# Sketched attention, a router and eight experts on one core: expert blocks in four waves beside the attention, in place of one pass behind it

## The chip, the core and the metric

One core of a Trainium2 chip runs the whole program. Its engines are TensorE (PE; PEld are its weight loads), VectorE (DVE), ScalarE (ACT), GpSimd (POOL) and SyncE (SP, which here only issues DMAs). The metric is the device time of one execution in microseconds: 638.33 us for the kernel before, the median of 3 runs (637.64 to 638.45). All data is float32.

## What is computed

Four batches of 1088 tokens with four heads of 32. `phi` maps a head's 32 numbers to 64 products of two 8-wide sketches; attention is `phi(q)` times the sum over tokens of `phi(k) v`, divided by `phi(q)` times the sum of `phi(k)`. The result, 4352 tokens of 128, goes to a noisy top-2 router, and each token to two of eight experts with a hidden width of 1024.

```python
q_p, k_p = (phi(q), phi(k))
num = np.einsum('bhsf,bhfd->bhsd', q_p, np.einsum('bhsf,bhsd->bhfd', k_p, v))
den = np.einsum('bhsf,bhf->bhs', q_p, np.sum(k_p, axis=2))[..., None] + 1e-06
x = (num / den).transpose(0, 2, 1, 3).reshape(B * S, H * D)
noisy_logits = x @ w_gate + np.log1p(np.exp(x @ w_noise)) * noise
top2 = np.argpartition(-noisy_logits, 2, axis=1)[:, :2]
...
h = np.maximum(x[mask] @ w1[e], 0.0)
out[mask] += top2_w[mask, k, None] * (h @ w2[e])
```

## The kernel before, in words

A batch is eight tiles of 128 tokens and a rest of 64; two rests make a tile, 34 tiles in all. `attention(b)` (L694) does one batch: `key_values` (L278) transposes the keys, multiplies them with the sketch, forms `phi` on DVE and the batch's `kv` matrix of 64 by 33 per head; `queries` (L324) does the same for four query tiles at a time and divides; `router` (L364) takes these four tiles, transposes them, multiplies with both router weights, picks the top two on DVE, counts the pairs per expert with two products (L435, L436), and POOL scatters each tile's two weighted copies into the DRAM tensor `xs`, at rows sorted by expert (L453). ScalarE needs an Exp and a Ln table in each call (L393, L395, L424). ACT's queue also clears the DRAM tensor `parts` (L236).

Behind the last of nine router calls, `table` (L458) works out on one partition which expert and which rows each block has: 23 blocks of 256 rows, 21 of 128, and four blocks of 256 of the fullest expert. `ends` (L552) writes eight pieces of padding. Then `blocks` (L617): SP fetches each block's rows and its expert's two matrices of 512 KB (`fetch`, L574; five buffers), TensorE transposes the rows (L596), multiplies with w1 into the PSUM bank `hp` (L673), DVE and ACT take turns to evict it with a ReLU, TensorE multiplies with w2 (L632), and POOL scatters the 128-row results into `parts` (L657). Two evicted groups wait in `later` before their second product is issued. When the four last blocks are under way, `combine` (L601) adds the two parts of each token and stores them, and the four blocks' own results are added to the output by accumulating scatters (L648).

Each engine runs its instructions in order. The framework's scheduler chooses that order at build time; each engine then waits on semaphores for what it reads and for buffers to come free.

## Time and profile before

| what | value |
|---|---|
| median of 3 runs | 638.33 us |
| the profiled execution: time, span | 637.79 us, 636.1 us |
| busy PE, PEld | 469.1 us (74%), 408.6 us (64%) |
| busy DVE, ACT, POOL | 198.5, 119.3, 174.7 us |
| DMA | 80.27 MB, mean 126 GB/s |
| mean granted TensorE clock | 0.80 |

The page gives shares over the whole span; since the span has two halves of a different kind, it is read by stretches. A PE matmul of float32 stands in the trace as two records and a transpose as one. The granted clock is a share of 2.4 GHz, so 0.50 is 1.2 GHz.

### The profile page before, as it was taken

What the parts mean: (1) busy time and instruction counts of PE and PEld (TensorE: products, weight loads), DVE (VectorE), ACT (ScalarE), POOL (GpSimd) and SP (SyncE); (2) the same over time, 40 slices, a digit from 0 to 9 for tenths busy, and PEclk for the clock granted to TensorE, in tenths of its full rate; (3) what the DMA queues carried; (4) which work ended last, traced back from release to release, by engine and by line L of the source; (5) the groups of instructions that cost most, each with busy time, mean ns of one, the idle gap of its engine ahead of it and who ended that gap; (6) DMA issues with size and microseconds to landing.
All of it is one profiled execution on the core that took longest, in us unless ns stands there. A gap on an engine that the chain in (4) does not pass through costs nothing.

```text
span 636.1 us, 8071 instructions
## 1 busy us (share of the span) xinstructions
PE 469.1 (74%) x2781; PEld 408.6 (64%) x2781; DVE 198.5 (31%) x687; ACT 119.3 (19%) x232; POOL 174.7 (27%) x236
## 2 busy tenths in 40 slices
PE   0278547847575757854518999999999999999950
PEld 0275337534563456423307999999999999999950
DVE  3112444152513451155371222222232222223430
ACT  0101330121203120132201222222212122221100
POOL 3300155106330524023420313232222313132016
PEclk9999575566557755656557999999999999999995
DMA  8841010001000100000129977868686867750753
GB/s 213 277 164 35 4 63 30 4 1 34 14 19 1 34 4 30 0 14 21 34 57 323 304 235 207 258 197 257 193 255 205 245 222 236 236 150 9 246 189 29
DMA packets 86296, 80.27 MB, mean 126 GB/s; under 512 B 11875, under 2 KB 76004, under 8 KB 85744
## 3 DMA queue, kind: packets, MB, share of 16 engines
q1 hardware_dynamic: 73152, 65.66, 33.5%
q0 software_dynamic: 5472, 8.96, 4.9%
q10 hardware_dynamic: 7632, 5.15, 2.5%
...
q14 instruction: 18, 0.15, 0.1%
HBM read 63.44 MB, written 16.75 MB: 126 GB/s over the span
## 4 chain that ended last, share of the span: by engine, by line
issue 36%; PE 28%; DVE 12%; POOL 9%; DMA 6%; ACT 5%; ACTq 2%; POOLq 1%; SPq 0%; DVEq 0%
POOL parts L657 8%; PE bank L336 5%; PE bank L304 5%; PE bank L255 4%; PE bank L337 4%; DMA two<-parts 3%; PE bank L374 3%; PE bank L350 2%; PE bank L331 2%; ACT L395 2%; DVE phk L249 1%; ACT qT L334 1%; POOL out_dram L648 1%; DVE x L358 1%; DVE phq L341 1%
## 5 line engine op out<-in xcount | busy, mean ns | idle before, releaser
L673 PE MATMUL hp<-bT,w 128*128 128x256 f32 (+1 forms) x768 | 157.9, 338 | 2.4 <-DMA w<-in_moe_w_dram 2.0
L632 PE MATMUL acc<-w,h 128*128 128x128 f32 x1200 | 158.2, 275 | 0.5 <-DVE h L588 0.5
L632 PEld LDWEIGHTS acc<-w,h 128*128 128x128 f32 x1200 | 154.2, 192 | 6.2 <-DVE h L588 0.6
L673 PEld LDWEIGHTS hp<-bT,w 128*128 128x128 f32 x768 | 116.5, 194 | 9.2 <-issue 2.4
L657 POOL DMA_INDIRECT parts<-y,xb x67 | 65.8, 983 | 196.6 <-DVE y L588 147.9
L453 POOL DMA_INDIRECT xs<-xg,to x68 | 69.3, 1019 | 160.5 <-issue 59.5
L588 DVE TENSOR_SCALAR h<-hp 128x512 f32<-128x512 f32 x80 | 55.2, 691 | 120.2 <-PE hp L673 120.2
L590 ACT ACTIVATE h<-hp 128x512 f32<-128x512 f32 x70 | 41.8, 597 | 123.9 <-PE hp L673 123.9
L435 PE MATMUL bank<-masks,earlier 128*128 128x32 f32 (+1 forms) x18 | 5.4, 394 | 62.5 <-DVE g L427 62.5
L435 PEld LDWEIGHTS bank<-masks,earlier 128*128 128x128 f32 x18 | 4.5, 312 | 63.2 <-issue 63.2
L255 PE MATMUL bank<-sk,kT 128*128 128x64 f32 x136 | 29.8, 419 | 11.8 <-ACT kT L290 11.3
L304 PE MATMUL bank<-vaug,phk 128*128 128x66 f32 x128 | 29.4, 424 | 12.3 <-DVE phk L249 12.3
L255 PEld LDWEIGHTS bank<-sk,kT 128*128 128x128 f32 x136 | 29.6, 333 | 12.5 <-ACT kT L290 11.7
L336 PE MATMUL bank<-qT,sq 128*128 128x512 f32 (+1 forms) x36 | 29.9, 928 | 9.8 <-ACT qT L334 9.7
L304 PEld LDWEIGHTS bank<-vaug,phk 128*128 128x128 f32 x128 | 27.9, 330 | 13.4 <-issue 9.8
L341 DVE TENSOR_TENSOR phq<-qa,bank 128x512 f32<-128x512 f32 (+1 forms) x18 | 11.8, 658 | 59.1 <-PE bank L337 58.9
L337 PE MATMUL bank<-qT,sq 128*128 128x512 f32 (+1 forms) x36 | 27.4, 857 | 0.0
L596 PE MATMUL bank<-ident,xb 128*128 128x128 f32 x75 | 16.3, 277 | 14.0 <-DMA xb<-xs 14.0
L350 PEld LDWEIGHTS bank<-kv,phq 128*128 128x128 f32 (+1 forms) x144 | 18.2, 201 | 10.3 <-DVE phq L341 4.7
L334 ACT COPY qT<-bank 128x512 f32<-128x512 f32 (+1 forms) x18 | 10.1, 562 | 76.6 <-PE bank L331 76.6
L588 DVE COPY bT<-bank 128x256 f32<-128x256 f32 x21 | 8.9, 425 | 42.7 <-PE bank L596 42.7
L350 PE MATMUL bank<-kv,phq 128*128 128x66 f32 (+1 forms) x144 | 19.0, 285 | 3.4 <-DVE phq L341 3.4
...
## 6 DMA issues: line engine op xcount, KB each, us to landing
w<-in_moe_w_dram SPq DMA_DIRECT2D x90, 512.0 KB, 4.7
...
kld<-in_k_dram SPq DMA_DIRECT2D x4, 512.0 KB, 4.9
vld<-in_v_dram SPq DMA_DIRECT2D x4, 512.0 KB, 4.0
qld<-in_q_dram SPq DMA_DIRECT2D x4, 512.0 KB, 4.4
...
```

What stands on the lines that cost most here:

```text
L255: nc.tensor.matmul(ps[:, c0:c0 + H * 2 * R], lhsT=kT, rhs=sk[:, i, :], start=(i == 0), stop=(i == 1))
L304: nc.tensor.matmul(o, lhsT=phk[:, t, hs, :].rearrange("p h f -> p (h f)"), rhs=vaug[:, hs, t, :], start=(t == 0), stop=False)
L336: nc.tensor.matmul(pa[:, 0:w], lhsT=sq[:, 0, :], rhs=qT[:, 0:w], start=True, stop=True)
L337: nc.tensor.matmul(pb[:, 0:w], lhsT=sq[:, 1, :], rhs=qT[:, 0:w], start=True, stop=True)
L350: nc.tensor.matmul(ps[rows, c0:c0 + 2 * A1], lhsT=phq[hp][:, P * i + rows.start:P * i + rows.stop], rhs=kv[:, hp, :], start=True, stop=True)
L374: nc.tensor.matmul(ps[:, 2 * E * i:2 * E * (i + 1)], lhsT=xT[:, P * i:P * (i + 1)], rhs=wgn[:], start=True, stop=True)
L453: disjoint("xs", nc.gpsimd.indirect_dma_start(out=xs[:], out_offset=bass.IndirectOffsetOnAxis(ap=to[:, t:t + 1], axis=0), in_=xg[:, t, :], ...
L588: nc.vector.tensor_scalar_max(o, i, 0.0) if relu else nc.vector.tensor_copy(o, i)
L590: nc.scalar.activation(out=o, in_=i, func=AF.Relu) if relu else nc.scalar.copy(o, i)
L632: nc.tensor.matmul(acc[:, D * c:D * (c + 1)], lhsT=h[:, P * (n * i + c):P * (n * i + c + 1)], rhs=w2[:, j, :], start=(j == 0 and c == 0), ...
L657: disjoint("parts", nc.gpsimd.indirect_dma_start(out=parts[:], out_offset=bass.IndirectOffsetOnAxis(ap=to[:, c, :], axis=0), in_=y[:, D * ...
L673: nc.tensor.matmul(hp[:, P * n * i:P * n * (i + 1)], lhsT=w1[:, P * (j0 + i):P * (j0 + i + 1)], rhs=xT[:, 0:P * n], start=True, stop=True)
```

## The change

The blocks are computed in four waves, each from a table of its own. After batch `b` is routed, `table` counts the pairs that came so far; a number of 128-row blocks is then sure to be full whatever the routing (at most 127 rows per expert are left over), and the wave computes that many: 9, 18, 16, and 32 with all the rest behind the last batch. The blocks are all of 128 rows, each with its own fetch of weights (75 instead of 45); there are four weight buffers, two `hp` banks instead of three, and one evicted group waits in `later` instead of two. `wave(0)` is issued behind attention 2, `wave(1)` behind attention 3, so that the scheduler can mix them.

```diff
+    def full_blocks(tiles):
+        return -(-(2 * P * tiles - E * (P - 1)) // P)
+    WAVES, used = [], 0
+    for d in DONE[:-1]:
+        WAVES.append(full_blocks(d) - used)
+        used += WAVES[-1]
+    LAST = (PAIRS + E * (P - 1)) // P - used
+    OLD = (2 * P * DONE[-2] - P * used + E * (P - 1)) // P
...
-    SP = [mybir.EngineType.SP]
-    IN_RANGE = "counts of pairs, clamped in the table"
-    def number(tab, at, most):
-        return nc.values_load(tab[0:1, at:at + 1], engines=SP, min_val=0, max_val=most,
-                              skip_runtime_bounds_check_because=IN_RANGE)
-    def ends(tab):
-        for e in range(E):
-            r = number(tab, 2 * (NB + NS) + 2 + e, E * CAP - P)
-            disjoint("xs", nc.sync.dma_start(xs[bass.ds(r, P), :], pad[:]))
...
-    def fetch(tab, k, n):
-        if k is not None:
-            e = number(tab, 2 * k, E - 1)
-            r = number(tab, 2 * k + 1, E * CAP)
-            return [(rows(r, n), *weights(e), n, False)]
-        e = number(tab, 2 * (NB + NS), E - 1)
-        r = number(tab, 2 * (NB + NS) + 1, E * CAP - 2 * P * NL)
-        w1, w2 = weights(e)
-        return [(rows(r + 2 * P * i, n), w1, w2, n, True) for i in range(NL)]
...
+    def wave(tab, step, K, spread, old=0):
+        fetched, ready, later = [], [], []
+        done = [0]
+        def fetch(i):
+            e = value(tab, 0, i, E - 1)
+            r = value(tab, 1, i, E * CAP)
...
+            w1 = wpool.tile([P, F], F32, name="w1", tag="w1")
+            w2 = wpool.tile([P, FJ, D], F32, name="w2", tag="w2")
+            nc.sync.dma_start(w1[:], moe_w1[bass.ds(e, 1), :, :].rearrange("o p f -> p (o f)"))
+            nc.sync.dma_start(w2[:], moe_w2[bass.ds(e, 1), :, :].rearrange("o (j p) d -> p (o j) d", p=P))
+            fetched.append((xb, w1, w2))
...
+        def second():
+            acc, h, w2, j0, xb = later.pop(0)
+            for i in range(4):
+                nc.tensor.matmul(acc[:, 0:D], lhsT=h[:, P * i:P * (i + 1)], rhs=w2[:, j0 + i, :],
+                                 start=(j0 + i == 0), stop=(j0 + i == FJ - 1))
+            if j0 + 4 < FJ:
+                return
+            y = ypool.tile([P, D], F32, name="y", tag="y")
+            evict(y[:], acc[:, 0:D], spread=spread)
+            disjoint("parts", nc.gpsimd.indirect_dma_start(
+                out=parts[:], out_offset=bass.IndirectOffsetOnAxis(ap=xb[:, D:XW].bitcast(U32), axis=0),
+                in_=y[:], in_offset=None, bounds_check=PAIRS - 1, oob_is_err=False), int(done[0] >= old))
+            done[0] += 1
...
+        fetch(0)
+        turn_input()
+        for b in range(K):
+            if b + 1 < K:
+                fetch(b + 1)
+            xb, w1, w2, xT, acc = ready.pop(0)
+            for j0 in range(0, FJ, 4):
+                hp = ps_h.tile([P, 512], F32, name="hp", tag="hp")
+                for i in range(4):
+                    nc.tensor.matmul(hp[:, P * i:P * (i + 1)], lhsT=w1[:, P * (j0 + i):P * (j0 + i + 1)],
+                                     rhs=xT[:], start=True, stop=True)
+                h = hpool.tile([P, 512], F32, name="h", tag="h")
+                evict(h[:], hp[:], relu=True, spread=spread)
+                later.append((acc, h, w2, j0, xb))
+                if len(later) > 1:
+                    second()
+                if j0 == 0 and fetched:
+                    turn_input()
+        while later:
+            second()
...
-    order = []
-    for i in range(max(NB, NS)):
-        order += [(i, 2)] * (i < NB) + [(NB + i, 1)] * (i < NS)
-    order.append((None, 2))
-    blocks(tab, order)
+    tabs = []
+    for b in range(B):
+        attention(b, b == 0)
+        tabs.append(table(DONE[b], WAVES[b] if b < B - 1 else LAST, b == B - 1))
+        if b >= LEAD:
+            wave(tabs[b - LEAD], b - LEAD, WAVES[b - LEAD], b == B - 1, WAVES[b - LEAD])
+    for b in range(B - LEAD, B - 1):
+        wave(tabs[b], b, WAVES[b], True, WAVES[b])
+    ends(tabs[-1], LAST)
+    wave(tabs[-1], B - 1, LAST, True, OLD)
+    for x in combining["going"]:
+        for _ in x:
+            pass
+    for x in combine(old_tokens, N, 1, 3):
+        for _ in x:
+            pass
```

Combining is done in two parts: the tokens of the first batches while wave 3 runs its newer blocks (`0 < old < K` in `second`), 1152 tokens at the end. The clearing of `parts`, the accumulating scatters and the doubled blocks of the fullest expert are gone.

```diff
+            if 0 < old < K and done[0] > old + 1:
+                todo = combining.setdefault("todo", None)
+                if todo is None:
+                    combining["todo"] = todo = combine(0, old_tokens, 0, G)
+                    combining["going"] = []
+                for x in combining["going"]:
+                    next(x, None)
+                if todo:
+                    combining["going"].append(todo.pop(0))
+                    next(combining["going"][-1])
...
-        for r0 in range(0, per, R_):
-            n = min(R_, per - r0)
-            two = cpool.tile([P, R_, 2, D], F32, name="two", tag="two")
-            behind(nc.sync.dma_start(two[:, 0:n], src[:, r0:r0 + n]), "parts")
-            one = cpool.tile([P, R_, D], F32, name="one", tag="one")
-            nc.vector.tensor_add(out=one[:, 0:n], in0=two[:, 0:n, 0, :], in1=two[:, 0:n, 1, :])
-            disjoint("out", nc.sync.dma_start(dst[:, r0:r0 + n, :], one[:, 0:n]))
...
+        def piece(r0, n):
+            two = work.tile([P, G, 2, D], F32, name="two", tag="phi", bufs=5)
+            behind("parts", nc.sync.dma_start(two[:, 0:n], src[:, r0:r0 + n]), step)
+            yield
+            V.tensor_add(out=two[:, 0:n, 0, :], in0=two[:, 0:n, 0, :], in1=two[:, 0:n, 1, :])
+            yield
+            disjoint("out", nc.sync.dma_start(dst[:, r0:r0 + n, :], two[:, 0:n, 0, :]))
+            yield
+        return [piece(r0, min(C, per - r0)) for r0 in range(0, per, C)]
```

Attention and router are rebuilt. Keys and queries share `features`: a transpose of four tiles of one head, one product with both halves of the sketch, an addition and the products on DVE. The queries' `phi` is transposed afterwards (`attend`), and `kv` is extended by its product with the router's weights, so that the router's logits come out of the same product as the numerators, and the transposes before the router are gone. One ScalarE table that holds Exp and Ln is loaded at the start. The router takes eight or nine tiles in one call (batch 0 in two calls of four): five calls instead of nine. Constants are loaded in two DMAs instead of eight.

```diff
+    def features(tiles, tag, by_head=False):
+        n = len(tiles)
+        ps = bank()
+        for i, x in enumerate(tiles):
+            nc.tensor.transpose(ps[:, P * i:P * (i + 1)], x, ident[:])
+        xT = work.tile([P, 512], F32, name="xT", tag="xT", bufs=3)
+        nc.scalar.copy(xT[:, 0:P * n], ps[:, 0:P * n])
+        ps = bank()
+        for i in range(n):
+            nc.tensor.matmul(ps[:, P * i:P * (i + 1)], lhsT=xT[:, P * i:P * (i + 1)],
+                             rhs=sk[:].rearrange("p i h r -> p (i h r)"), start=True, stop=True)
+        two = ps[:, 0:P * n].rearrange("p (a i b y) -> p a i b y", a=n, i=2, b=H)
+        ab = work.tile([P, G, H, 2, R], F32, name="ab", tag="ab", bufs=3)
+        o = ab[:, 0:n].rearrange("p a b w r -> p b a (w r)" if by_head else "p a b w r -> p a b (w r)")
+        nc.scalar.copy(o, two[:, :, 1])
+        V.tensor_tensor(out=o, in0=two[:, :, 0], in1=o, op=ALU.add)
+        phi = work.tile([P, G, H, RR], F32, name=tag, tag="phi", bufs=5)
+        th = ab[:, 0:n].rearrange("p t h w r -> p (t h) w r")
+        V.tensor_tensor(
+            out=phi[:, 0:n].rearrange("p t h (i j) -> p (t h) i j", i=R),
+            in0=th[:, :, 0, :].unsqueeze(3).to_broadcast([P, H * n, R, R]),
+            in1=th[:, :, 1, :].unsqueeze(2).to_broadcast([P, H * n, R, R]), op=ALU.mult)
...
-            for i in range(n):
-                nc.tensor.transpose(ps[:, P * i:P * (i + 1)],
-                                    qx[:, t0 + i, hp, :, :].rearrange("p c x -> p (c x)"), ident[:])
-            qT = work.tile([P, 512], F32, name="qT", tag="qT")
-            nc.scalar.copy(qT[:, 0:w], ps[:, 0:w])
-            pa, pb = bank(), bank()
-            nc.tensor.matmul(pa[:, 0:w], lhsT=sq[:, 0, :], rhs=qT[:, 0:w], start=True, stop=True)
-            nc.tensor.matmul(pb[:, 0:w], lhsT=sq[:, 1, :], rhs=qT[:, 0:w], start=True, stop=True)
-            qa = work.tile([P, 512], F32, name="qa", tag="qa")
-            nc.scalar.copy(qa[:, 0:w], pa[:, 0:w])
-            ph = work.tile([P, 512], F32, name=f"phq{hp}", tag=f"phq{hp}")
-            nc.vector.tensor_mul(out=ph[:, 0:w], in0=qa[:, 0:w], in1=pb[:, 0:w])
-            phq.append(ph)
...
+        ps = bank()
+        for hp in range(2):
+            nc.tensor.transpose(ps[0:KC, P * hp:P * (hp + 1)], kv[:, hp, 0:KC], ident[:])
+        kvT = work.tile([KC, 2 * P], F32, name="kvT", tag="kvT")
+        nc.scalar.copy(kvT[:], ps[0:KC, 0:2 * P])
+        ps = bank()
+        for hp in range(2):
+            nc.tensor.matmul(ps[:, 2 * E * hp:2 * E * (hp + 1)], lhsT=kvT[:, P * hp:P * (hp + 1)], rhs=wgn[:, hp, :],
+                             start=(hp == 0), stop=True, skip_group_check=True)
+        both = ps[:, 0:4 * E].rearrange("p (a x) -> p a x", a=2)
+        V.tensor_copy(kv[upper, :, KC:KC + 2 * E], both[upper, :, :])
+        nc.scalar.copy(kv[lower, :, KC + 2 * E:YC], both[lower, :, :])
...
+        for hp in range(2):
+            ps = bank()
+            for i in range(n):
+                nc.tensor.transpose(ps[:, P * i:P * (i + 1)], two_heads(phi, i, hp), ident[:])
+            t = work.tile([P, 512], F32, name="phT", tag="phT", bufs=4)
+            nc.scalar.copy(t[:, 0:P * n], ps[:, 0:P * n])
+            phT.append(t)
+        for i0 in range(0, n, 2):
+            m = min(2, n - i0)
+            ps = bank()
+            for i in range(i0, i0 + m):
+                for rows, kv in kvs_of[i]:
+                    for hp in range(2):
+                        c0 = 2 * YC * (i - i0) + YC * hp
+                        nc.tensor.matmul(
+                            ps[rows, c0:c0 + YC], lhsT=phT[hp][:, P * i + rows.start:P * i + rows.stop],
+                            rhs=kv[:, hp, :], start=True, stop=True)
+            nc.scalar.copy(nd[:, at + i0:at + i0 + m].rearrange("p t a y -> p (t a y)"), ps[:, 0:2 * YC * m])
...
+        V.tensor_scalar_add(den, nd[:, 0:n, :, DH:DH + 2], 1e-6)
+        V.reciprocal(den, den)
+        sc = small.tile([P, MOST, H, 2 * E], F32, name="sc", tag="sc")[:, 0:n]
+        V.tensor_tensor(
+            out=sc.rearrange("p t h y -> p (t h) y"),
+            in0=nd[:, 0:n, :, KC:YC].rearrange("p t a (h y) -> p (t a) h y", h=2),
+            in1=den.rearrange("p t a h -> p (t a) h").unsqueeze(3).to_broadcast([P, 2 * n, 2, 2 * E]),
+            op=ALU.mult)
+        V.tensor_add(out=sc[:, :, 0:2, :], in0=sc[:, :, 0:2, :], in1=sc[:, :, 2:4, :])
+        lz = t3("lz", 2 * E)
+        V.tensor_add(out=lz, in0=sc[:, :, 0, :], in1=sc[:, :, 1, :])
+        logits, z = lz[:, :, 0:E], lz[:, :, E:2 * E]
...
-        ps = bank()
-        for i in range(n):
-            nc.tensor.transpose(ps[:, P * i:P * (i + 1)], x[:, i, :, :].rearrange("p h d -> p (h d)"), ident[:])
-        xT = work.tile([P, 512], F32, name="xT", tag="xT")
-        nc.scalar.copy(xT[:, 0:w], ps[:, 0:w])
-        ps = bank()
-        for i in range(n):
-            nc.tensor.matmul(ps[:, 2 * E * i:2 * E * (i + 1)], lhsT=xT[:, P * i:P * (i + 1)],
-                             rhs=wgn[:], start=True, stop=True)
```

Three places of the new order, beside the old one. TensorE, in the middle of the program: before, the tail of the first batch's router and the start of the second batch (`kx` keys, `qx` queries).

```order
L374 MATMUL bank<-wgn,xT 128x16 x4
L435 MATMUL bank<-masks,earlier 128x32
L288 MATMUL bank<-ident,kx 128x128 x7
L436 MATMUL bank<-before,ones 128x32
L288 MATMUL bank<-ident,kx 128x128
L255 MATMUL bank<-sk,kT 128x64 x16
L304 MATMUL bank<-vaug,phk 128x66 x8
L306 MATMUL bank<-vaug_rest,phk_rest 128x66
```

Now, in attention 2 (`vld_106` its values, `kv_172` its matrix, `w_1265`, `w_1266` and `w_1281` weights of wave 0's first two blocks):

```order
L670 MATMUL hp<-bT,w_1265 128x128
L352 MATMUL bank<-vld_106,phk 128x96 x8
L352 MATMUL bank<-v_rest,rest_phi_995 128x96 x2
L640 MATMUL acc<-w_1266,h 128x128 x3
L362 MATMUL bank<-ident,kv_172 66x128 x2
L640 MATMUL acc<-w_1266,h 128x128
L670 MATMUL hp<-bT,w_1281 128x128 x2
L367 MATMUL bank<-wgn,kvT 128x16 x2
L304 MATMUL bank<-ident,qld 128x128 x4
L670 MATMUL hp<-bT,w_1281 128x128 x2
L640 MATMUL acc<-w_1266,h 128x128
L465 MATMUL side<-masks,earlier 128x72
```

Between the products of one batch's attention stand first-layer (L670) and second-layer (L640) groups of wave 0, and a counting product of the router before (L465).

TensorE, late in the blocks (numbers are weight buffers). Before, first-layer (L673) and second-layer (L632) groups alternate, each second-layer group of four behind another first-layer group:

```order
L673 MATMUL hp<-bT,w_3077 128x128 x4
L632 MATMUL acc<-w_3030,h 128x128 x4
L596 MATMUL bank<-ident,xb 128x128 x2
L673 MATMUL hp<-bT,w_3077 128x128 x4
L632 MATMUL acc<-w_3030,h 128x128 x4
L673 MATMUL hp<-bT,w_3135 128x256 x2
L632 MATMUL acc<-w_3078,h 128x128 x4
```

Now, in the last wave, a block's eight first-layer products stand together, and its eight second-layer ones right behind them:

```order
L632 MATMUL acc<-ident,xb 128x128
L670 MATMUL hp<-bT,w_4439 128x128 x8
L640 MATMUL acc<-w_4440,h 128x128 x8
L632 MATMUL acc<-ident,xb 128x128
L670 MATMUL hp<-bT,w_4486 128x128 x8
L640 MATMUL acc<-w_4487,h 128x128 x8
```

POOL: before, all scatters of routed rows (L453) stand ahead of all scatters of block results (L657):

```order
L453 DMA xs<-xg_1625,to_1623 36096x129 x4
L453 DMA xs<-xg_1637,to_1635 36096x129 x4
L453 DMA xs<-xg_1753,to_1751 36096x129 x2
L453 DMA xs<-xg_1763,to_1761 36096x129 x2
L657 DMA parts<-y,xb 8704x128 x67
L648 DMA out_dram<-y,tok 4352x128 x8
```

Now the results of wave 0's second and third block (L646) stand behind the last of the 18 scatters of batch 1 (`xg_898`, `xg_904`), and batch 2's follow behind the next two:

```order
L501 DMA xs<-xg_898,to 35968x129
L501 DMA xs<-xg_904,to 35968x129
L646 DMA parts<-y,xb 8704x128 x2
L491 COPY xg_1892<-pair 128x9
L491 COPY xg_1898<-pair 128x9
L646 DMA parts<-y,xb 8704x128 x2
L501 DMA xs<-xg_1196,to 35968x129
L501 DMA xs<-xg_1202,to 35968x129
```

A block's input buffer, which its result's scatter reads for the row numbers, is free only when that scatter is done.

## Rows read from the trace of the kernel before

**Rows 1.** The page, part 2: the span in 40 slices of 15.9 us.
```profile
PE   0278547847575757854518999999999999999950
...
PEclk9999575566557755656557999999999999999995
DMA  8841010001000100000129977868686867750753
```

**Rows 2.** Windows: stretch, length, busy per engine (instructions), granted clock, DMA share, GB/s.
```profile
104.00:128.00 24.00, 18.99 (x72) 14.28 (x72) 4.12 (x6) 2.93 (x5) 7.77 (x10) 0.58 0.05 17
312.00:332.00 20.00, 2.04 (x9) 1.80 (x8) 15.25 (x106) 3.37 (x6) 6.15 (x7) 0.50 0.17 50
344.28:360.00 15.72, 15.72 (x127) 15.28 (x126) 4.04 (x7) 3.52 (x7) 2.97 (x3) 1.00 1.11 342
360.00:370.93 10.93, 10.93 (x85) 10.52 (x84) 2.92 (x5) 2.32 (x5) 2.95 (x3) 1.00 0.77 239
```

**Rows 3.** Timeline of PE, small block of the steady stretch: start us, us, instructions.
```profile
388.99 1.06 PE L673 MATMUL hp<-bT,w 128*128 128x128 f32 x8
389.89 1.06 PE L632 MATMUL acc<-w,h 128*128 128x128 f32 x8
390.78 0.38 PE L596 MATMUL bank<-ident,xb 128*128 128x128 f32 x2
```

**Rows 4.** Timeline of all engines, first 40 us, idle before in brackets.
```profile
9.29 0.18 DVE L103 TENSOR_SCALAR expo<-words 128x16 uint32<-128x16 uint32 x1 [8.26 <-DMA words<-in_S_dram]
...
18.84 1.97 PE L288 MATMUL bank<-ident,kx 128*128 128x128 f32 x8 [0.74 <-POOL kx L282]
...
32.08 7.09 PE L255 MATMUL bank<-sk,kT 128*128 128x64 f32 x32 [11.27 <-ACT kT L290]
```

**Rows 5.** Timeline, the first router call (four tiles).
```profile
66.23 0.19 DVE L392 SCALAR_TENSOR_TENSOR u<-zs 128x32 f32<-128x32 f32 x1 [3.56 <-ACT zs L391]
...
66.70 1.28 ACT L395 ACT_TABLE_LOAD   x1
...
76.35 0.17 DVE L446 CAST to<-at 128x4 uint32<-128x4 f32 x1
```

**Rows 6.** Timeline of POOL, scatters of the routed rows.
```profile
78.43 0.97 POOL L453 DMA_INDIRECT xs<-xg,to  x1 [0.30 <-issue]
79.70 0.96 POOL L453 DMA_INDIRECT xs<-xg,to  x1 [0.30 <-issue]
```

**Rows 7.** DMA issues: line, count, KB each, median us to landing.
```profile
w<-in_moe_w_dram SPq DMA_DIRECT2D x90, 512.0 KB, 4.7
...
xb<-xs SPq DMA_DIRECT2D x21, 64.5 KB, 4.7
xs<-xg,to POOLq DMA_INDIRECT x68, 2.3
```

**Rows 8.** Timeline of SP's queue behind the table.
```profile
321.79 6.41 SPq L555 DMA_DIRECT2D xs<-pad  x8
332.26 0.42 SPq L568 DMA_DIRECT2D xb<-xs  x1
...
334.66 0.34 SPq L568 DMA_DIRECT2D xb<-xs  x1
```

**Rows 9.** Timeline, eviction of the group that starts at 388.99.
```profile
390.15 0.60 ACT L590 ACTIVATE h<-hp 128x512 f32<-128x512 f32 x1 [2.44 <-PE hp L673]
```

**Rows 10.** The chain that ended last, its end: start us, us, releaser.
```profile
588.39 2.25 DMA parts<-y,xb
590.78 3.88 DMA two<-parts
...
614.48 2.00 DMA out_dram<-one
```

**Rows 11.** Source line 392, one instruction per router call.
```profile
L392 DVE SCALAR_TENSOR_TENSOR u<-zs x9: 191/192/240, 66.2 to 312.7; 128x32 f32<-128x32 f32 x8, 128x16 f32<-128x16 f32 x1
```

766 lines of the change are left out of this document (347 added, 419 removed).

## The prediction

> **What bounds the kernel now.** I read the slices of the span first, then the stretches, then the order of time inside three of them. The slices fall in two halves [rows 1]: up to about 330 us TensorE is busy half to three quarters of the time at a granted clock around 0.6 and the DMA engines are nearly idle; behind it TensorE is full at 1.0 and the DMA engines work. The stretches say the same with numbers [rows 2]: 0.58 while attention runs, 0.50 while the one table is made and TensorE has 2 us of work in 20, 1.00 in the expert blocks. The first half is thus a chain of short steps, the second is TensorE's own pace. The change can gain by putting blocks under the chain, and by a shorter chain; it can't gain in the blocks' own pace.
>
> The pace of a block: groups of four matmuls of 128 columns follow each other at 0.90 and 0.89 us [rows 3]; a 128-row block is four such groups and a transpose of 0.11, so 4 x 0.89 + 0.11 = 3.67 us. Three units (a 256-row and a 128-row block) take 10.93 us [rows 2], 3.64 each: cutting 256 into 128 costs TensorE next to nothing. That is at 2.4 GHz. In the first 40 us the same instructions take twice that: eight transposes 1.97, 16 matmuls (32 records) 7.09 us, so 0.246 and 0.443 each [rows 4]; that is 1.2 GHz, though the slices print 1.0 there, so I go by the durations.
>
> **The change part by part.** Both kernels compute 75 units of 128 rows (before 27 x 2 + 21; after 9 + 18 + 16 + 32). Before, all of them stand behind the table. After, TensorE's order has attention 0 and 1 alone, then wave 0 mixed into attention 2, wave 1 into attention 3, then waves 2 and 3.
>
> (a) Until the first block. The DVE starts its sketch constants at 9.29 us, when eight small loads on ACT have landed [rows 4]; two loads are left, I take 5.5, and first transposes at 10.5. Attention 0 and 1 are 74 transposes and 115 matmuls in the new order: 74 x 0.246 + 115 x 0.443 = 69 us at 1.2 GHz, 35 at 2.4. With some 8 us for the hops of two key chains (copy, transpose, copy, product, copy) that is 10.5 + 69 + 8 = 88. The other condition gives the same: the first four tiles' numerators are there at about 45; a router call takes 10.3 us from its first step to its row numbers for four tiles [rows 5], 2 x 1.28 of it table loads that the one preloaded table removes, but two calls now share DVE with attention 1's features, so the second ends near 70. Then eight scatters at 1.27 [rows 6] behind the first eight, 2.3 to land [rows 7], an input block of 4.7: 70 + 10.2 + 2.3 + 4.7 = 87. I take **88**; ends 68 (2.4 GHz throughout, only the chain) and 105 (1.2 GHz, and TensorE waits at each of the five router products that the order puts between attention 1's). All else that attention loses (the expanded query copies on POOL, the clearing of the parts by 4.4 MB from ACT's queue, the transposes before the router) is inside this count, not beside it.
>
> (b) TensorE's work from there on: 75 x 3.67 = **275**, and attention 2 and 3, 72 transposes and 115 matmuls at 2.4 GHz (half of 0.246 and 0.443), **34**.
>
> (c) Waits inside that, which are mine to choose. In attention 2 TensorE's order holds 17 us of attention and 10 us of blocks, but DVE has router 1, table 1 and ten feature products: a router call of nine tiles between 10.3 and 20.6 us, I take 16, some 5 for a table (DVE's whole load in the 20 us around the old, wider one was 15.25 [rows 2]), 8 for features, and the chain's ends: 40 us in all, so 13 wait. Attention 3 starts behind wave 0 with router 2 done: 6 wait. POOL has block 1's output behind router 1's 18 scatters (18 x 1.27 = 23 us), and wave 1's first input needs a buffer which that output frees: 4. A new wave starts with an empty pipeline, 1.5 each, and the last one behind eight padding writes which take 6.41 us on SP [rows 8] and are only just covered by the four weight buffers: 4 + 3. From the middle of wave 2 the order puts the two first-layer groups ahead of the two second-layer groups; an eviction on ACT starts 0.26 behind the group's end and takes 0.60 [rows 9], on DVE 0.09 more, against 0.89 of cover: about 0.15 in some 40 blocks, 6. Combining the older tokens inside wave 3 moves 4.9 MB, 14 us at 342 GB/s [rows 2], over seven blocks that leave 0.2 us each: 8 after the prefetch lead. Sum **44**, ends 25 and 75.
>
> Feeding the blocks: 75 loads of weights instead of 45, each block 1.05 MB of weights, 0.066 in and 0.066 out: 1.18 MB. Before's own burst moves 342 GB/s for 16 us with TensorE full [rows 2], so 3.45 us per block against 3.67: it hides, by little. SP issues a fetch every 2.4 us [rows 8], which hides too. With 3.67 at 2.4 GHz, the price is nothing as long as the DMA engines give over 321 GB/s. Here a rule of the Trainium skill speaks against the change: "DMA: Bandwidth & Descriptors", section Bandwidth, asks for transfers of 1 MiB and more, and its section on the anatomy of a DMA puts 2.0 us of fixed cost on each. As an estimate from that page, two loads of 512 KB one behind the other would be 6.4 us per block, and the sum some 200 us more. The row says otherwise, since it shows the same 512 KB loads overlapping; I follow the row.
>
> (d) The end. Before, 614 to 636 are eight accumulating scatters; after, the last block's output goes to the parts (0.5 for the copy), from scatter to load 2.25, loads of three pieces 3.9, a store 2.0 [rows 10], an add and issues between: **12** instead of some 22.
>
> Sum: 88 + 275 + 34 + 44 + 12 = 453 us of span. The profiled execution of before had 636.1 of span in 637.79, so 1.7 around it; its time is 0.5 below the median of 638.33, which I leave aside: **455 us**.
>
> **The rivals.**
> 1. The front is quicker: TensorE reaches 2.4 GHz in attention 0 and 1, or half my waits aren't there. For it: no clearing on ACT's queue; against it: 0.58 all through the attention of before [rows 2]. 455 - 20 - 10 = 425.
> 2. The blocks are bound by DMA. Before's steady stretch ran 239 GB/s at 0.77 busy [rows 2], 310 at full; midway between 239 and 342 is 290, 4.07 us per block, 0.4 more in the 64 blocks with no attention beside them: 455 + 25 = 480. Against it: the burst; for it: the burst was short.
> 3. The overlap doesn't come: the in-order engines make the mixed waves wait for attention and the reverse. A batch takes 61.6 us now (eight router calls in 246.5 us [rows 11], two per batch); both mixed stretches at that, with 10 us of blocks each, instead of 40 and 33: 455 + 70 = 525. For it: one TensorE queue, router products in the middle of blocks; against it: nothing in a block depends on the attention beside it.
> 4. Slower: TensorE stays at 1.2 GHz. If every wave has short gaps (late weights, router products), the blocks run at the pace that attention has now. Then (b) doubles, 309 more, and takes up most of (c): about 730. It decides from a mean granted clock of 0.63: 88 + 309 / 0.63 + 44 + 12 + 2 = 637. For it: attention with TensorE 0.79 busy was granted 0.58 [rows 2]; against it: blocks back to back were granted 1.00 without a break. "TensorE: Matmul & The Clock Gate" of the Trainium skill, section on HAM oscillation, describes this case, bursts of matmuls between waits for weights that each run cold; the blocks of before, fed by the same loads, don't show it.
>
> **How the numbers follow.** The forecast 0.64 (its own range 435 to 475), rival 1 0.11, rival 2 0.15, rival 3 0.07, rival 4 0.02, and 0.01 for what lies between 3 and 4, near no change. The range 424 to 500 takes in the first three and leaves rivals 3 and 4 out. A measurement of this kernel tells changes of about 0.2% from none. Faster: 0.64 + 0.11 + 0.15 + 0.07 = 0.97; the same 0.01; slower 0.02.
>
> **What would show it.** Right: the first expert transpose near 88 us; a granted clock at 1.0 from some 130 us to the end; PE full in 40-us stretches with DMA at 300 GB/s or more; blocks 3.7 to 3.9 us apart; wave 3 starting near 305. Wrong: block starts over 4 us apart with TensorE waiting for weights (rival 2); TensorE idle on features or on router products for over 30 us between 88 and 190 (rival 3); a clock near 0.6 in waves (rival 4); or POOL's outputs behind the scatters holding input buffers for more than the 4 us that I gave them.

## The result, and the profile after

The changed kernel takes **434.41 us** (median of 4 runs, 433.68 to 435.31) where the kernel before took 637.99 beside it (636.92 to 638.45): ratio 0.681, 95% interval 0.679 to 0.683. 455 was forecast, with 424 to 500. The same kernel took 494.8 us (ratio 0.771, 0.766 to 0.776) when it ran again among the experiments, with the kernel before unchanged at 639.7; that gap of 60 us is the subject of half the experiments. Times are medians of all executions of a run, one of 1317 us in e7 among them whose cause isn't known; ratios leave out the slow executions, those over 1.5% above the fastest.

The page of the run at 434, span and slices of 10.8 us, for [rows 1]:

```profile
span 433.5 us, 9044 instructions
...
PE   1878782999998999998999999999999999889980
...
PEclk9999796899999999999699999999999999999995
DMA  6193012974959289893999999699999979999915
```

From the eighth slice to the last but one TensorE is 0.8 busy or more, at a granted clock of 0.8 or more but for the twentieth. Stretches of it (columns as in [rows 2]):

```profile
60.00:80.00 20.00, 11.09 (x77) 10.00 (x77) 6.52 (x28) 5.83 (x15) 9.76 (x13) 0.74 0.37 111
100.00:140.00 40.00, 37.64 (x324) 36.29 (x323) 20.24 (x87) 16.22 (x40) 30.99 (x33) 1.00 0.78 244
140.00:180.00 40.00, 39.36 (x338) 37.60 (x337) 24.64 (x88) 13.92 (x36) 19.39 (x19) 1.00 0.71 215
200.00:220.00 20.00, 17.27 (x128) 16.84 (x127) 3.63 (x8) 3.19 (x7) 9.47 (x10) 0.83 0.85 267
220.00:260.00 40.00, 39.67 (x353) 39.27 (x352) 10.52 (x21) 8.90 (x21) 10.81 (x11) 1.00 1.07 339
360.00:380.00 20.00, 17.81 (x144) 16.73 (x145) 6.35 (x13) 3.69 (x10) 5.50 (x5) 1.00 1.05 347
```

From 100 us on TensorE works 37 to 40 us of each 40; only 200 to 220 and the combining from 360 to 400 fall below 18 of 20. At 220 to 260 the DMA engines move 339 GB/s beside a full TensorE, and no block waits for a load.

TensorE's way to the first block (timeline: start, us, idle before in brackets), for [rows 4]:

```profile
10.41 2.08 PE L309 MATMUL bank<-sk,xT 128*128 128x128 f32 x8 [0.68 <-ACT xT L306]
...
26.80 1.16 PE L309 MATMUL bank<-sk,xT 128*128 128x128 f32 x8 [0.73 <-ACT xT L306]
...
36.61 0.60 PE L304 MATMUL bank<-ident,kld 128*128 128x128 f32 x4
...
66.17 0.66 PE L304 MATMUL bank<-ident,kld 128*128 128x128 f32 x4
74.99 0.47 PE L632 MATMUL acc<-ident,xb 128*128 128x128 f32 x1 [8.16 <-DMA xb<-xs]
```

Eight records of a feature product take 2.08 us at 10 and 1.16 at 27: TensorE was at half speed first and at full speed from some 25 us on, in attention 0, though the page prints 1.00 for both. It fell back to half speed twice before the blocks ran: from 48 to 56 (granted 0.57, four transposes 1.09 in place of 0.60 or 0.66) and from 75, behind the 8.2 us wait, to 80. Attention 0 ends at 36.6, attention 1 at 66.2, and then TensorE waits 8.2 us for the first block's rows. POOL says why, for [rows 6]:

```profile
49.47 1.16 POOL L501 DMA_INDIRECT xs<-xg,to  x1 [30.20 <-DVE noisy L455]
...
61.67 0.96 POOL L501 DMA_INDIRECT xs<-xg,to  x1 [0.30 <-issue]
...
70.58 0.97 POOL L501 DMA_INDIRECT xs<-xg,to  x1 [0.30 <-issue]
```

Sixteen scatters follow each other, most of them every 1.27 us, from 49.5 to 71.6. The ninth, the first of the router's second call, starts at 61.67 without a wait: its row numbers had been there since 56.5 (DVE, L484). The last lands at 72.9, the rows are in at 74.9.

Blocks, for [rows 3]. Middle of wave 2, then wave 3, then wave 3 beside the combining:

```profile
242.18 0.83 PE L670 MATMUL hp<-bT,w 128*128 128x128 f32 x6
242.85 0.27 PE L632 MATMUL acc<-ident,xb 128*128 128x128 f32 x1
242.96 0.39 PE L670 MATMUL hp<-bT,w 128*128 128x128 f32 x2
...
307.28 2.05 PE L670 MATMUL hp<-bT,w 128*128 128x128 f32 x16
309.19 1.64 PE L640 MATMUL acc<-w,h 128*128 128x128 f32 x12
310.67 0.27 PE L632 MATMUL acc<-ident,xb 128*128 128x128 f32 x1
...
359.48 0.27 PE L632 MATMUL acc<-ident,xb 128*128 128x128 f32 x1
360.11 2.05 PE L670 MATMUL hp<-bT,w 128*128 128x128 f32 x16 [0.35 <-ACT bT L608]
...
363.94 0.27 PE L632 MATMUL acc<-ident,xb 128*128 128x128 f32 x1
```

From transpose to transpose it is 3.68 (to 246.54), then 4.01 (from 306.66), then 4.46. In the last, the transpose stands behind all of the second layer and the next first layer waits 0.35 for its eviction.

### The profile page after: what moved, and what is told of

Read it like the earlier page. It is cut to its first block, busy times and chain, and to the rows that moved or that the text cites. A ratio compares the mean times of both kernels' runs of the same rounds, so it can differ in the third digit from the quotient of the medians.

```text
span 433.5 us, 9044 instructions
## 1 busy us (share of the span) xinstructions
PE 382.2 (88%) x3089; PEld 363.8 (84%) x3089; DVE 165.4 (38%) x564; ACT 113.3 (26%) x274; POOL 153.5 (35%) x208
## 4 chain that ended last, share of the span: by engine, by line
PE 55%; issue 16%; POOL 9%; DMA 9%; DVE 7%; ACT 2%; SPq 1%; POOLq 0%; ACTq 0%; DVEq 0%
PE hp L670 19%; PE acc L640 18%; POOL xs L501 5%; PE bank L309 5%; POOL parts L646 4%; PE bank L352 4%; PE bank L392 3%; DMA xs<-xg,to 3%; DMA w<-in_moe_w_dram 2%; PE bank L304 2%; DMA xb<-xs 2%; PE acc L632 1%; DMA two<-parts 1%; DMA parts<-y,xb 1%; PE bank L381 1%
## 5 line engine op out<-in xcount | busy, mean ns | idle before, releaser
L670 PE MATMUL hp<-bT,w 128*128 128x128 f32 x1200 | 163.6, 281 | 6.3 <-ACT bT L608 3.6
L640 PE MATMUL acc<-w,h 128*128 128x128 f32 x1200 | 164.3, 282 | 0.1
L670 PEld LDWEIGHTS hp<-bT,w 128*128 128x128 f32 x1200 | 148.3, 194 | 12.0 <-ACT bT L608 8.5
L640 PEld LDWEIGHTS acc<-w,h 128*128 128x128 f32 x1200 | 148.6, 193 | 2.4 <-ACT h L608 0.3
L646 POOL DMA_INDIRECT parts<-y,xb x75 | 75.1, 1002 | 189.7 <-DVE y L606 124.7
L606 DVE COPY y<-acc 128x128 f32<-128x128 f32 x66 | 19.1, 290 | 103.8 <-PE acc L640 96.1
L608 ACT COPY bT<-acc 128x128 f32<-128x128 f32 x75 | 20.0, 266 | 117.3 <-PE acc L632 114.2
L632 PE MATMUL acc<-ident,xb 128*128 128x128 f32 x75 | 21.3, 284 | 12.5 <-DMA xb<-xs 12.0
L309 PE MATMUL bank<-sk,xT 128*128 128x128 f32 x136 | 24.3, 326 | 6.5 <-ACT xT L306 6.5
L309 PEld LDWEIGHTS bank<-sk,xT 128*128 128x128 f32 x136 | 20.4, 226 | 9.7 <-ACT xT L306 9.6
L632 PEld LDWEIGHTS acc<-ident,xb 128*128 128x128 f32 x75 | 10.7, 142 | 14.3 <-DMA xb<-xs 8.4
L315 DVE TENSOR_TENSOR ab<-bank,ab 128x256 f32<-128x256 f32 (+1 forms) x20 | 7.6, 380 | 36.7 <-ACT ab L314 36.6
L392 PE MATMUL bank<-kv,phT 128*128 128x98 f32 (+1 forms) x144 | 18.4, 279 | 1.5 <-ACT phT L383 1.5
L352 PE MATMUL bank<-vld,phk 128*128 128x96 f32 x128 | 17.6, 297 | 0.3 <-DVE phk L318 0.3
L352 PEld LDWEIGHTS bank<-vld,phk 128*128 128x128 f32 x128 | 16.9, 213 | 0.8 <-DVE phk L318 0.5
L306 ACT COPY xT<-bank 128x512 f32<-128x512 f32 (+1 forms) x20 | 10.5, 523 | 10.3 <-PE bank L304 9.6
```

The lines of the kernel that those rows point to most:

```text
L306: nc.scalar.copy(xT[:, 0:P * n], ps[:, 0:P * n])
L309: nc.tensor.matmul(ps[:, P * i:P * (i + 1)], lhsT=xT[:, P * i:P * (i + 1)], rhs=sk[:].rearrange("p i h r -> p (i h r)"), start=True, stop= ...
L352: nc.tensor.matmul(ps[:, W * hp:W * (hp + 1)], lhsT=lhsT, rhs=rhs, start=(t == 0 and hp == 0), stop=(t == NT), skip_group_check=True)
L392: nc.tensor.matmul(ps[rows, c0:c0 + YC], lhsT=phT[hp][:, P * i + rows.start:P * i + rows.stop], rhs=kv[:, hp, :], start=True, stop=True)
L606: V.tensor_scalar_max(o, i, 0.0) if relu else V.tensor_copy(o, i)
L608: nc.scalar.activation(out=o, in_=i, func=AF.Relu) if relu else nc.scalar.copy(o, i)
```

## The experiments

They ran on the chips with the numbers 2 (e1 to e6), 7 (e7 to e9), 10 (e10, e11) and 9 (e12); on which chip the run above ran isn't known. They also ran later, so what is said below of a chip could be the time's doing as well. Ratios are to the kernel before, timed on the same chip in the same rounds.

**e1, the order of waves 2 and 3 pinned as the code has it** (waves 2 and 3; the products of L640 and L670 are pinned in the same way).

```diff
+        keep = tc.keep_in_program_order if pin else (lambda i: i)
...
-            nc.tensor.transpose(acc[:, P:2 * P], xb[:, 0:D], ident[:])
+            keep(nc.tensor.transpose(acc[:, P:2 * P], xb[:, 0:D], ident[:]))
...
```

> Edit: in waves 2 and 3 TensorE's instructions keep the order of the code, in which first-layer and second-layer groups of four alternate and the next block's transpose stands between them; nothing else changes. Theory (the order costs): in the changed kernel a block takes 3.68 us where groups alternate and 4.01 where eight first-layer products stand together, since the eviction is then uncovered; 27 blocks of 4.01 give back 9 us, and the ten blocks beside the combining (45.6 us from 355.0 to 400.6) go to some 39 in place of 45.6. 434.4 becomes 417 to 421. Rival (DMA binds in the last wave): 32 blocks at 1.18 MB, 0.5 MB of padding and 5 MB of combining are 43 MB, 125 us at the 347 GB/s of that stretch, as long as the wave takes now; then the same time goes to waits for weights, and the total stays above 429.

505.6 us, ratio 0.790 (0.786 to 0.795): 11 more than the unedited kernel there (e5); theory and rival were both reckoned from the run at 434. In the code's order the transpose follows the group that ends a bank's use, and waits for its eviction, 4.34 us per block:

```profile
301.80 0.33 PE L634 MATMUL acc<-ident,xb 128*128 128x128 f32 x1 [0.44 <-DVE y L606]
...
306.14 0.33 PE L634 MATMUL acc<-ident,xb 128*128 128x128 f32 x1 [0.44 <-DVE y L606]
```

So a block's pace does follow the order, but this was the wrong order; e6 mends it.

**e2, no overlap** (all four waves behind the loop over attention, pinned; padding behind wave 2's loads).

```diff
-        if b >= LEAD:
-            wave(tabs[b - LEAD], b - LEAD, WAVES[b - LEAD], b == B - 1, WAVES[b - LEAD])
-    for b in range(B - LEAD, B - 1):
-        wave(tabs[b], b, WAVES[b], True, WAVES[b])
...
+    for b in range(B - 1):
+        wave(tabs[b], b, WAVES[b], b > 0, WAVES[b], pin=True)
```

> Edit: all four waves stand behind all four attentions on TensorE, with groups alternating in all of them (so it is compared with e1_alternate, not with the changed kernel). Theory (the gain comes from the shorter attention, and the overlap hides little): attention 1 takes 30 us alone in the changed kernel (36.6 to 66.2), attention 2 and 3 will take 30 to 35 each, so the first block starts at 127 to 137, 75 blocks at 3.68 are 276, and with some 6 of wave starts and 13 of tail the total is 422 to 434: 5 to 15 more than e1_alternate. Rival (the overlap is the bulk of the gain): a batch alone takes the 61.6 us that it took before the change, the first block starts near 190, the total is 480 or more, over 60 above e1_alternate.

531.2 us, 0.832 (0.827 to 0.836), some 25 more than e1. The first block starts at 166.0, where before it started at 334.6. Attention 2 takes 38 us alone and attention 3 42, both with TensorE near half speed for most of the time (windows, granted clock 0.60 and 0.67) and attention 3 with two late completions (8 us), and TensorE then waits 17 us for router 3:

```profile
69.08 1.12 PE L304 MATMUL bank<-ident,kld 128*128 128x128 f32 x4
...
107.05 0.60 PE L304 MATMUL bank<-ident,kld 128*128 128x128 f32 x4
...
148.49 0.73 PE L392 MATMUL bank<-kv,phT 128*64 128x98 f32 x8 [0.92 <-issue]
...
166.00 0.47 PE L635 MATMUL acc<-ident,xb 128*128 128x128 f32 x1
```

```profile
69.00:107.00 38.00, 29.38 (x148) 25.90 (x148) 21.64 (x86) 9.41 (x24) 6.68 (x11) 0.60 0.43 129
107.00:149.00 42.00, 29.96 (x159) 25.91 (x158) 20.97 (x88) 10.43 (x28) 18.82 (x21) 0.67 0.09 29
```

So the first block moves up by 169 us without any overlap: attention and router take about 40 per batch and not 61.6 [rows 11], and the last table isn't waited for by all blocks. The 25 lie between the theory's 5 to 15 and the rival's 60, but they aren't the overlap's worth. The late completions told of under e5 weigh on this pair unequally: ACT waits 66 us for them in e1 (sum of the table of waits) and 26 in e2. And e2 pins the slow order in waves 0 and 1 too, which e1 doesn't: their 27 blocks come 4.25 to 4.41 us apart in e2, so some 16 of the 25 can be the order's (27 times 0.6, the step from 3.68). The first makes the overlap look smaller than it is, the second larger; what it is worth wasn't measured. The two traces show the size of it: in the run at 434, the 101 us from 75 to 176 hold all of attention 2 and 3 and the products of some 15 blocks; in e2, attention 2 and 3 and the last router take 97 us without a block.

**e3, more buffers.**

```diff
-    xpool = ctx.enter_context(tc.tile_pool(name="xpool", bufs=8))
-    ypool = ctx.enter_context(tc.tile_pool(name="ypool", bufs=6))
+    xpool = ctx.enter_context(tc.tile_pool(name="xpool", bufs=16))
+    ypool = ctx.enter_context(tc.tile_pool(name="ypool", bufs=14))
```

> Edit: 16 input buffers for blocks in place of 8, and 14 output buffers in place of 6; nothing else. Theory (input buffers are held by outputs queued on POOL behind the 18 scatters of batch 3, so SP's fetch comes late at 203 us): the two blocks at 199 to 212.6 us, which take 13.4 us in place of 7.4, are back at 3.68 each, without the half-speed clock behind the wait: 6 us, and up to 2 more at other fetches that waited; 434.4 becomes 426 to 429. Rival (the fetch waits for something else, the weight buffers or the scattered rows): no change, 433 to 436.

496.0, 0.771 (0.764 to 0.778): as e5. But the wait that it was to remove isn't in e5's profile either (in the run at 434, SP waits 30.8 us for results to leave input buffers; here that row is missing, and TensorE is late itself). It stays open what the buffers are worth.

**e4, the first block later on TensorE.**

```diff
+            if step == 0:
+                tc.add_manual_dep(t_.ins, last_of[LEAD].ins.name, ORDER, reason="behind the key chain")
```

> Edit: on TensorE the first block's transpose stands behind the key-value product of attention 2, in place of ahead of most of it; nothing else. Theory (the 8.2 us in which TensorE waits for the first block's rows, 66.8 to 75.0, are filled with attention 2's key features and products): 5 to 8 us less, 426 to 430, and the clock doesn't fall in that stretch. Rival (attention 2's own chain on DVE, with the router of batch 1, sets the end of the mixed stretch, so the wait moves there): under 2 us less, 432 to 435.

494.8 (485.3 to 497.7; no ratio), as e5 (490.0 to 495.6): no gain shown. Again the wait isn't there to be filled: in e5 attention 1 itself ends at 78.3, and the first block's transpose follows at 79.2 without a wait for its rows. Open for the same reason.

**e5, no edit.**

> The changed kernel without an edit, to be compared with e1 to e4, which all came out between 494 and 531 us, and in which TensorE's completions reach ACT and SP up to 15 us late while POOL issues the 18 scatters of a batch (e3_pools has the very same order of instructions on every engine as the changed kernel). Theory (a property of the chip or the time that those four ran at, not of their edits): this kernel too takes 485 to 510 here, with TensorE idle for 10 us and more at a time in the bursts of 18 scatters. Rival (the edits did it, through other buffer addresses): 432 to 437 as in the profile after the change.

494.8, 0.771 (0.766 to 0.776). Theory held: the time comes with this chip, or the time at which it ran, and not with an edit. Wave 2's first transpose is at 287.0 in place of 225.7, and from there to the last transpose both runs take the same 190 us (287.0 to 477.2, 225.7 to 416.7): the 61 us lie ahead of wave 2. Four of them are there before the first scatter, which starts at 53.5 in place of 49.5: the feature products at 28 and 32 still take 2.08 us, where the run at 434 had 1.16. The other 57 lie in the stretch with the 68 scatters of routed rows. TensorE, ACT and SP in the first burst beside blocks, and POOL's part:

```profile
106.49 1.08 PE L640 MATMUL acc<-w,h 128*128 128x128 f32 x8
...
113.67 1.58 PE L670 MATMUL hp<-bT,w 128*128 128x128 f32 x8
...
131.18 0.48 PE L632 MATMUL acc<-ident,xb 128*128 128x128 f32 x1 [12.67 <-ACT y L608]
...
110.47 0.27 ACT L608 COPY y<-acc 128x128 f32<-128x128 f32 x1 [2.40 <-remote]
...
130.37 0.60 ACT L608 ACTIVATE h<-hp 128x512 f32<-128x512 f32 x1 [12.86 <-remote]
...
110.46 0.38 SPq L626 DMA_DIRECT2D w<-in_moe_w_dram  x1
...
130.40 0.38 SPq L626 DMA_DIRECT2D w<-in_moe_w_dram  x1
...
109.73 0.97 POOL L501 DMA_INDIRECT xs<-xg,to  x1 [0.30 <-issue]
...
126.27 1.00 POOL L646 DMA_INDIRECT parts<-y,xb  x1 [0.30 <-issue]
```

Second-layer products that the trace puts at 106.5 to 107.6 release ACT's copy and SP's next load together at 110.46, 2.9 us late, and the first-layer group of 113.67, recorded as done by 115.3, releases ACT's next eviction at 130.37, with SP's load again at the same moment. The trace has no event that released them ("remote"). The ends of matmuls are modelled, so it can't be told whether the products or their signals were late. All waits without a releaser are for results or buffers of TensorE; between DVE, ACT and POOL there is none.

**e6, the transpose inside the first-layer group.**

```diff
+                    if pin and j0 == 4 and i == 3 and fetched:
+                        turn_input()
...
-                if j0 == 0 and fetched:
+                if j0 == 0 and fetched and not pin:
```

> Edit: as e1_alternate, but the next block's transpose stands between the third and the fourth product of the second first-layer group, where it stands in the blocks that took 3.68 us; in e1_alternate it stood behind the second-layer group that frees its PSUM bank, and waited 0.44 for that bank's eviction, 4.34 per block. Theory (the order alone sets a block's pace): blocks of waves 2 and 3 at 3.68 to 3.75, where the changed kernel has 4.01, and at most 4.0 beside the combining where it has 4.46; 15 to 20 us less than the changed kernel in the same session. Rival (DMA binds in the last wave): blocks wait for weights, less than 5 us gained.

487.4, 0.764 (0.759 to 0.770), 7 less than e5; the intervals overlap a little, so the gain rests on the traces: from wave 2's first transpose to the last it takes 183.8 in place of 190.3. In waves 2 and 3, 33 of the 47 steps from block to block take 3.68 or 3.69, at 310 to 350 GB/s, so DMA feeds that pace. Less than expected, because eight blocks beside the combining take 38.6 us, 9.1 more than at 3.68; TensorE waits there for rows, 5.1 us in all, and for weights, 1.3:

```profile
414.18 0.30 PE L634 MATMUL acc<-ident,xb 128*128 128x128 f32 x1 [0.51 <-DMA xb<-xs]
...
425.38 0.30 PE L634 MATMUL acc<-ident,xb 128*128 128x128 f32 x1 [1.24 <-DMA xb<-xs]
```

In 420 to 440 the DMA engines moved 371 GB/s at a share of 1.09. Theory for the blocks alone, rival for the combining's stretch.

**e7, plain writes on ACT's queue in place of scatters.** The rows go to fixed places and aren't sorted by expert, so e7 and e11 don't compute the result; they price the scatters and aren't kernels to use.

```diff
-                disjoint("xs", nc.gpsimd.indirect_dma_start(
-                    out=xs[:], out_offset=bass.IndirectOffsetOnAxis(ap=to[:, i, t:t + 1], axis=0),
...
+                m = 2 * (t0 + t) + i
+                r0 = m % E * CAP + m // E * P
+                disjoint("xs", nc.scalar.dma_start(xs[r0:r0 + P, :], xgs[i][:, t, :]), step)
```

> Edit: the routed rows go to DRAM by plain writes of whole tiles from ACT's queue, at fixed rows, in place of the 68 scatters on POOL; blocks read fixed tiles and the padding is at fixed rows (so a block's rows are not those of its expert; the same number of rows, bytes and blocks). Compared with e5_same_again, 494.8, where TensorE's completions reach ACT and SP 2.5 to 15 us late in the bursts of scatters. Theory (POOL's scatters themselves delay the completions): without them no idle TensorE of 10 us beside the attention, 410 to 440 in all. Rival (the writes of 516-byte rows do it, or the chip alone whatever the kernel does): the same stretches stay idle, over 470.

460.6, 0.720 (0.717 to 0.723), and no late completion at all, on the chip on which e9, with its scatters, has them. The time misses the theory's 410 to 440 and rules out the rival's 470; the idle time that is left is the edit's own: ACT stands in front of its writes, and TensorE waits for it (table of waits: total, times, longest):

```profile
ACT bT L608 <- DMA xs<-xg: 29.2, 2, 17.6
```

**e8, the kernel before.**

> The kernel before, without an edit, for its profile on this chip, since its time here (639) is that of the first session while the changed kernel's is 60 us longer. Theory (the late completions come with scatters issued while TensorE works without a break): before's scatters, eight at a time and beside DVE's router, delay completions too, but TensorE waits there for DVE anyway, so the span is within 2 us of 636 and TensorE's busy time in 60 to 330 us is unchanged. Rival (its shorter bursts cause no late completion at all): no wait of ACT or SP for a completion that is over 1 us late.

639.6, span 637.9 (one profile). Its waits show no completion without a releaser. The rival: in this profile bursts of eight, beside a TensorE that is 0.6 busy, delay nothing.

**e9, all combining at the end** (the edit is to e6).

```diff
-    wave(tabs[-1], B - 1, LAST, True, OLD, pin=True)
+    wave(tabs[-1], B - 1, LAST, True, 0, pin=True)
...
-    for x in combine(old_tokens, N, 1, 3):
+    for x in combine(0, N, 1, G):
```

> Edit: as e6_alternate_inside, but all combining stands behind the last block. Compared with e6, 487.4. Theory (beside the blocks the combining costs what DMA can't move: 9 us, eight blocks of 38.6 in place of 29.4 in e6): the wave gets 9 us shorter, and the 2944 older tokens at the end cost 4.5 MB at some 340 GB/s, 13 us, so 2 to 6 us slower than e6. Rival (combining beside blocks is free in e6, the waits come from the weights alone): 11 us or more slower than e6.

494.5, 0.774 (0.770 to 0.779), 7 more than e6 but on another chip, so the traces decide. Wave 3 takes 113.8 from first to last transpose in place of 124.1, what follows the last transpose 34.0 in place of 18.0. So combining costs 10.3 us beside the blocks and 16.0 behind them, 5.7 more there: the theory's 2 to 6, and not the rival's 11. (The tokens that moved are 3200, 4.9 MB, and not the expectation's 2944.)

**e10, gaps on POOL behind the scatters of batches 2 and 3.**

```diff
+                if step >= 2:
...
+                    for g_ in range(3):
+                        gap = nc.gpsimd.memset(fill[:], 0.0)
+                        tc.add_manual_dep(gap.ins, s_.ins.name, ORDER, reason="behind the scatter")
```

> Edit: behind each of the 36 scatters of batches 2 and 3 POOL clears a scratch tile three times (some 1.4 us), and results of blocks may go between them; batches 0 and 1 keep their bursts, as a control in the same run; 16 input and 11 output buffers for blocks, so that the longer queue holds none. Compared with e5_same_again (494.8), where the bursts of batch 2 (140 to 170 us) and batch 3 (225 to 255) cost TensorE some 20 us each in late completions. Theory (it takes scatters back to back to delay completions): no completion over 1 us late beside batches 2 and 3, those of batch 1 as in e5; 450 to 465. Rival (each scatter delays by itself, or as long as scatters are under way): the same waits or longer ones beside batches 2 and 3, 490 or more.

461.7, 0.725 (0.721 to 0.729): 33 less than e5, across two chips. The surer comparison is inside the run, batch 1 against batches 2 and 3. Windows, e5 above and e10 below:

```profile
100.00:140.00 40.00, 22.73 (x161) 21.23 (x160) 15.57 (x75) 9.91 (x24) 20.74 (x23) 0.79 0.40 117
140.00:180.00 40.00, 23.85 (x158) 22.43 (x158) 4.71 (x32) 8.38 (x21) 20.47 (x21) 0.74 0.57 165
```

```profile
100.00:140.00 40.00, 24.47 (x164) 23.33 (x162) 15.79 (x77) 8.72 (x22) 22.44 (x26) 0.70 0.44 130
140.00:180.00 40.00, 39.46 (x338) 37.73 (x337) 12.49 (x24) 16.13 (x42) 36.17 (x51) 1.00 0.61 188
```

The burst of batch 1, left as it was, costs as much as in e5; that of batch 2, with three clearings (1.7 us) between its scatters, nothing any more. The larger buffers aren't the cause: e3 had 16 and 14 and took 496. Two late pairs are left, at 199 (4.6 and 4.0 us) and 268 (4.4 and 4.7), against the theory's none, and they stand behind five and seven scatters of block results in a row:

```profile
262.38 0.98 POOL L655 DMA_INDIRECT parts<-y,xb  x1 [0.31 <-issue]
...
266.25 0.98 POOL L655 DMA_INDIRECT parts<-y,xb  x1 [0.30 <-issue]
267.53 0.98 POOL L655 DMA_INDIRECT parts<-y,xb  x1 [0.30 <-issue]
...
268.25 0.27 ACT L617 COPY bT<-acc 128x128 f32<-128x128 f32 x1 [4.44 <-remote]
```

**e11, plain writes on POOL's queue** (the edit is to e7).

```diff
-                disjoint("xs", nc.scalar.dma_start(xs[r0:r0 + P, :], xgs[i][:, t, :]), step)
+                disjoint("xs", nc.gpsimd.dma_start(xs[r0:r0 + P, :], xgs[i][:, t, :]), step)
```

> Edit: as e7_direct_rows (plain writes of whole tiles at fixed rows, fixed tiles read, fixed padding), but issued from POOL's queue in place of ACT's. e7 had no late completion at all. Theory (descriptors that POOL writes by itself delay the completions, scattered or not): late completions of ACT and SP as in e5, over 470. Rival (only the scatters with an index per row do it): none over 1 us late, 420 to 445, faster than e7 (460.6), since ACT's queue no longer waits in front of a write.

421.5, 0.660 (0.658 to 0.661), two executions, on the chip on which e10's batch 1 has its late completions. The rival: POOL's plain writes (0.54 us each) delay nothing. The one late pair (3.8 and 2.6 us, at 184) comes, once more, behind six results scattered in a row from 175 to 182.

**e12, together**, all parts shown above, with one clearing between the scatters of batch 1.

> Edit: the order of e6 in waves 2 and 3; the first blocks of waves 0 and 1 behind the key products of attention 2 and 3 as in e4; the buffers of e10; and between any two scatters, those of routed rows of batches 1 to 3 and of results of waves 0 to 2, one to three clearings of a scratch tile on POOL. e10 (461.7) still had late completions beside batch 1 (12.2 and 3.8 us, with half-speed products behind them, some 20 in all) and behind five and seven results in a row (4.6 and 4.4, some 8 each with the clock). Theory (no row of scatters back to back, no late completion): 36 us less idle TensorE beside the attention, 7 for the order of waves 2 and 3 (e6 against e5), less some 10 for the later rows of batch 1: 425 to 440. Rival (the gaps of one clearing, 0.5 us, in batch 1 are too short): late completions stay beside batch 1, 445 to 460.

454.1, 0.707 (0.703 to 0.710), 41 less than the unedited kernel in e5 on another chip, the lowest of the versions that keep the scatters on these chips (e10 was at 461.7). It lies in the rival's 445 to 460, but not by the rival's mechanism: beside the bursts with gaps no wait of ACT, DVE or SP lacks its releaser. Two do (0.15 and 0.85 us) in batch 0's burst, which has no gaps. But that burst of sixteen, and five results scattered in a row without gaps (337 to 343), show no longer delay on this chip either, so e12 doesn't show that one clearing (0.5 us) is enough. The theory's time was missed because POOL is now full:

```profile
120.00:240.00 120.00, 114.70 (x985) 110.53 (x984) 49.74 (x156) 35.04 (x85) 107.73 (x158) 1.00 0.85 259
240.00:320.00 80.00, 65.94 (x521) 64.15 (x520) 15.35 (x31) 13.68 (x32) 70.32 (x110) 0.91 0.82 250
```

```profile
DVE y L622 <- DMA parts<-y,xb: 36.9, 9, 6.0
```

From 240 to 320 results leave behind batch 3's scatters and gaps, outputs hold their buffers, and most blocks come 4.5 to 7.6 us apart. Fewer or shorter gaps there weren't tried.

## Why the prediction was right, and where it was off

**Mechanism.** In the run on record blocks fill TensorE from the first block at 75 us on, at a granted clock of 1.00 from some 81 us but for 199 to 213, and rivals 2 to 4 didn't come: 339 GB/s beside a full TensorE, DVE no bound, blocks at 3.68. The sum came out 20 high, in two terms; rival 1 (425) came in part, with full speed in most of attention 0 and 1 and two of the waits missing. On chip 2 the kernel took 495, and that this lies in the range too is luck: the range reached that far for rival 2, loads that are too slow, and the time came from another mechanism, which no part of the prediction had.

**(a) 88, measured 75.** Two steps failed. "At 1.2 GHz": TensorE had full speed from some 25 us, but for 48 to 56, while 0.58 all through before's attention [rows 2] had been carried over; attention 0 and 1 end at 66.8 with 8.6 as the start in place of 10.5. And "the second call ends near 70, then eight scatters": the second call's row numbers were there before POOL was through with the first eight, so the condition was POOL's sixteen scatters from 49.5, and the rows took 1.84 to land, not 4.7. That both conditions gave the same 87 and 88 was chance, and hid that neither was right.

**(b) 309 holds**: 3.68 to 3.69 per block where the groups alternate, and attention 2 and 3 took 36 on TensorE, 2 of it by half speed, where 34 was forecast.

**(c) 44, measured 37** (421.3, the last eviction, less 75.0, less 309). The parts, from the transposes' starts:

| part | forecast | measured |
|---|---|---|
| attention 2 waits for DVE | 13 | 0.7; and 2.3 lost by half speed behind the 8.2 us wait |
| attention 3 | 6 | none seen |
| input buffers behind POOL's scatters | 4, wave 1's start | 1.6 there, 6.1 at 199 to 213 beside batch 3's scatters, half of it half speed |
| starts of waves | 7 | 2 |
| order L1 L1 L2 L2 | 6 | 9, steps of waves 2 and 3 outside the combining; 21 of them take 0.33 more, not 0.15 in 40 |
| combining | 8 | 8.8 in ten blocks |

The rest, 6 to 7, lies mostly in the mixed stretches. The first two were the mis-sized ones. For attention 2 the forecast had 40 us of DVE work in a row; DVE was busy 2.3 us from 66 to 75 and 19.5 from 75 to 102, some 22. And TensorE hardly waits for what was left: wave 0's evictions are all on ACT, and router 2's counting product, in the middle of the blocks, waits 0.71 us at 111. The third, POOL's results behind the scatters, came out at 7.7 in place of 4, the prediction's last sign of being wrong; SP's wait for input buffers shows it (table of waits):

```profile
SPq L621 <- DMA parts<-y,xb: 30.8, 3, 15.0
```

Most of SP's wait is covered. At 203.2, behind the first result's scatter after batch 3's, SP issues the load, and TensorE waits 2.17 us for the rows until 205.2. Wave 3 started at 287 (305 forecast).

**(d) 12, measured 12.2** (421.3 to 433.5): landing 2.1, load of the parts 4.6, then additions and stores.

**Against the rule of the Trainium skill.** Loads of 512 KB gave 339 to 371 GB/s when several were under way (339 from 220 to 260 us above, 371 in e6). The Trainium skill's "DMA: Bandwidth & Descriptors", section Bandwidth, asks for 1 MiB and more; from that page's 2.0 us of fixed cost, which stands there for DMAs that GpSimd issues, the prediction had estimated some 200 us more. These loads are issued by SP, take a median of 6.1 us to land and come two to a block of 3.7 us; the trace doesn't bear the estimate out for overlapping loads, as the row before had said.

**What the forecast didn't contain.** Late completions: 57 of the 61 us that e5 loses lie in the stretch that has them. The last line of "what would show it" had results behind scatters in view, as a matter of buffers; that scatters in a row could delay TensorE's signals was in no rival. No row of before shows it, and e8's profile, on a chip that has it with the changed kernel, shows none either.
